# A depthwise causal convolution into a bilinear feed-forward: w3 transposed by DMA out of a bf16 copy in HBM instead of by TensorE

## The chip, the core and the metric

One core of a Trainium2 chip runs the whole kernel in one launch. The metric is device time in microseconds (us); less is better. The engines are named as in the profile: PE (TensorE, matmuls), PEld (its weight loads), DVE (VectorE), ACT (ScalarE), POOL (GpSimd) and SP (SyncE). POOL and SP also issue DMAs; what they issue runs on the same 16 DMA engines. In the profile POOL's DMAs are queue q0 and SP's are queue q1.

## The reference

```
w   = softmax(weight, axis=-1)                       # weight [8 heads, 7 taps]
y[b, s, h, g] = sum_k w[h, k] * xpad[b, s + k, h, g] # x [8, 3904, 192], 6 zero rows ahead; 192 = 8 heads x 24
X   = y.reshape(31232, 192)
out = (((X @ w1) * (X @ w2)) @ w3) @ w_out           # w1, w2 [192, 1024]; w3 [1024, 1024]; w_out [1024, 192]
```

All inputs and the output are float32. Because nothing nonlinear stands between `w3` and `w_out`, the kernel multiplies them first: W = w3 @ w_out, [1024, 192], and `out = (a * b) @ W`.

## The kernel before

The 31232 tokens are two halves (r = 0, 1) of 15616, worked on together. A half is cut in two ways. For the convolution it is cut into windows of 64 input rows that give 58 output rows each; 272 windows stand in ten blocks of 10, 10, 10, 32, 36, 36, 36, 36, 36 and 30 windows (`SIZES`). For the products it is cut into 31 rounds of 512 tokens.

- **`load_x(b)`** loads block b from HBM to SBUF, casting to bf16, by DMAs in POOL's queue. There are six buffers `xb`; blocks from 3 on use two each.
- **`conv(b, h0, nh)`** is the convolution of heads as matmuls with a band matrix, from `xb` into PSUM (`cps`), and copies it to `convo`. `conv_two` does two heads, and after the last two of a block calls `store(b)`.
- The feature dimension has to come onto the partitions. Blocks 0 to 2 are transposed on PE (`pe_transposes`). From window 26 on, `store` writes `convo` to a table `rows` in HBM (SP's queue), and `transposes(R)` reads it back for round R by three DMA transposes, also in SP's queue, into `xT`. `send(last)` issues the transposes of all rounds up to `last` whose rows are stored.
- **`first_product(R)`** makes a and b for the 8 groups `ft` of 128 features, 12 matmuls each; ACT copies a (`asb`), DVE multiplies it with b into `abT`. `abT` has three buffers.
- **`second_product(R, r)`** multiplies `abT` by W and writes 512 rows of `out` through ACT and SP.
- PSUM is one ring of four buffers (`banks`), taken in program order by every user.

The order of the work is written out by hand (a manual schedule). The start: 18 dummy matmuls (`warm`), the band matrix, block 0, `first_product(0)` with block 1 inside, `first_product(1)` with block 2 inside, `first_product(2)`. Then comes what is called the **W stage** below: for each of the eight row groups `jt` of w3, eight PE transposes of 128x128 (L404), their copy out of PSUM (L407, ACT and DVE in turn), and eight matmuls with `w_out` (`w3_product`, L413); the eight heads of block 3 are put between. After it stand the phases: phase 0 has four second products (rounds 0 and 1), each later phase two first products and then four second products. Block 4 and later blocks put four heads into a phase: a pair after the first second product (place 0) and a pair after the last (place 3).

POOL's queue in the start is: x of block 0, w1 and w2 up to column 768, x of block 1, copies that swap the halves of w1 and w2 (L332), the rest of w1 and w2, x of block 2, twelve more swap copies, `w_out`, eight loads of w3 (`w3b`, 128 rows each, cast to bf16), x of block 3, x of block 4. Each of POOL's DMAs signals one of eight semaphores in turn, and POOL waits for the DMA eight places earlier before it reuses one. From block 5 on a load is held back by a tiny copy (`pace`) that waits for a piece of `abT`.

Of the kernel before, what the change touches and what calls it, by code (L numbers as in the profile page):

```python
# [9 lines left out]
BF16 = mybir.dt.bfloat16  # L10
# [6 lines left out]
def kernel(  # L17
# [51 lines left out]
    def banks_bf16(name):  # L69
        return psum.tile([128, 16, 128], BF16, tag="banks", name=name)  # L70
# [18 lines left out]
    def load_x(b, parts=(0, 1)):  # L89
        tiles = xb_of.setdefault(b, [])  # L90
        zeros_of = zero_rows.setdefault(b, [])
        for i0, n in [v for e, v in enumerate(halves_of(b)) if e in parts]:
            xb = work.tile([128, n, D], BF16, tag="xb", bufs=6, name="xb")
            w = 0
            if i0 == 0:
                nc.vector.memset(xb[:, 0, :], 0.0)
                for r in range(NS):
                    nc.gpsimd.dma_start(out=xb[Q * r:Q * r + Q, 1:n, :], in_=x_spans(r, 1, n - 1))
                w = n
            while w < n:  # L100
                i = i0 + w
                m = min(n - w, WB - i % WB)
                at_end = i + m == NWIN
                if at_end:
                    m -= 1
                if m:
                    for r in range(NS):
                        nc.gpsimd.dma_start(out=xb[Q * r:Q * r + Q, w:w + m, :],  # L108
                                            in_=x_spans(r, i, m))
                if i % WB == 0:  # L110
                    zeros_of += [(xb, 0, w), (xb, 1, w)]
                w += m
                if at_end:
                    nc.gpsimd.memset(xb[Q:128, w, :], 0.0)
                    t = tok(NWIN - 1) - PAD
                    nc.gpsimd.dma_start(out=xb[0:Q, w, :], in_=x_rows[t:t + Q, :])
                    nc.gpsimd.dma_start(out=xb[Q:Q + PAD + LAST, w, :],
                                        in_=x_rows[TS + t:TS + t + PAD + LAST, :])
                    w += 1
            if len(halves_of(b)) == 1:  # L120
                tiles += [(xb, 0), (xb, SIZES[b] // 2)]
            else:
                tiles.append((xb, 0))
# [43 lines left out]
    def warm(n, t=None):  # L167
        t = banks("warm") if t is None else t
        for j in range(n):
            nc.tensor.matmul(t[:, j % 2, :], zeros[:, 0:128], zeros, start=True, stop=True)  # L170

    warm(18)


    wmax = const.tile([128, H], FP32)
# [153 lines left out]
    def swap_w(k, part, engines):  # L329
        cs = slice(WC[part], WC[part + 1])  # L330
        for f, (d, e) in zip(engines, ((0, Q), (Q, 0))):
            f(out=wsw[k][d:d + Q, cs], in_=wn[k][e:e + Q, cs])  # L332
# [7 lines left out]
    def first_product(R, between=None, lead=0):  # L340
        N = width(R)
        ab = work.tile([128, JT, NS, CH], BF16, tag="abT", bufs=LAG + 1, name="abT")
        abT_of[R] = ab
        r0 = (R * CH) % RING
        for ft in range(JT):
            pq = []
            for i in range(2):
                p = banks("pa" if i == 0 else "pb")
                pq.append(p)
                if ft == 0 and i == 0:  # L350
                    warm(lead, p)
                for k in range(NP):
                    for r in range(NS):
                        rs = slice(Q * r, Q * r + Q)
                        nc.tensor.matmul(  # L355
                            p[:, r, 0:N], w_of(i, k, r)[rs, ft * 128:(ft + 1) * 128],
                            xT[k][rs, r0:r0 + N],
                            start=(k == 0), stop=(k == NP - 1))
            pa, pb = pq
            asb = work.tile([128, NS, CH], BF16, tag="asb", bufs=3, name="asb")  # L360
            nc.scalar.copy(out=asb[:, :, 0:N], in_=pa[:, :, 0:N])  # L361
            nc.vector.tensor_tensor(out=ab[:, ft, :, 0:N], in0=asb[:, :, 0:N],  # L362
                                    in1=pb[:, :, 0:N], op=ALU.mult)
            if between and ft in between:
                between[ft]()

    def second_product(R, r):
        ab = abT_of[R]
        ng = width(R) // 128
        ops = banks("ops")  # L370
        for g in range(ng):
            for jt in range(JT):
                nc.tensor.matmul(  # L373
                    ops[:, g // 2, (g % 2) * D:(g % 2) * D + D],
                    ab[:, jt, r, g * 128:(g + 1) * 128], W_sb[:, jt, :],
                    start=(jt == 0), stop=(jt == JT - 1))
        osb = slot([128, ng, D], FP32, "osb")
        nc.scalar.copy(out=osb.rearrange("p (a g) d -> p a (g d)", g=2),  # L378
                       in_=ops[:, 0:ng // 2, 0:2 * D])
        t0 = r * TS + R * CH  # L380
        nc.sync.dma_start(
            out=out[t0:t0 + ng * 128, :].rearrange("(g p) d -> p g d", p=128), in_=osb)
        if r == 1:
            del abT_of[R]
# [1 line left out]

    W_sb = const.tile([128, JT, D], BF16)
    wo_b = const.tile([128, JT, D], BF16)
    w3r = moe_w3.rearrange("(jt jp) g -> jp jt g", jp=128)
    wor = moe_w_out.rearrange("(gt gp) d -> gp gt d", gp=128)  # L390
    w3b_of, w3T_of = {}, {}

    def load_wo():
        nc.gpsimd.dma_start(out=wo_b, in_=wor)

    def load_w3(jt):
        w3b_of[jt] = stage.tile([128, DFF], BF16, tag="w3b", bufs=JT, name="w3b")
        nc.gpsimd.dma_start(out=w3b_of[jt], in_=w3r[:, jt, :])

    def w3_transpose(jt, f):  # L400
        w3b = w3b_of.pop(jt)
        tps = banks_bf16("w3ps")
        for gt in range(JT):
            nc.tensor.transpose(out=tps[:, gt, :], in_=w3b[:, gt * 128:(gt + 1) * 128],  # L404
                                identity=ident)
        w3T_of[jt] = stage.tile([128, JT, 128], BF16, tag="w3T", bufs=3, name="w3T")
        f(out=w3T_of[jt], in_=tps[:, 0:JT, :])  # L407

    def w3_product(jt):
        w3T = w3T_of.pop(jt)  # L410
        wps = banks("wps")
        for gt in range(JT):
            nc.tensor.matmul(wps[:, 0, 0:D], w3T[:, gt, :], wo_b[:, gt, :],  # L413
                             start=(gt == 0), stop=(gt == JT - 1))
        nc.scalar.copy(out=W_sb[:, jt, :], in_=wps[:, 0, 0:D])

# [17 lines left out]
    for k, f in ((0, V), (1, A), (2, V)):  # L434
        move(f, pe_transpose(0, k))
    swap_w(1, 0, (V, A))
    load_x(2)
    for k in (0, 2, 1):
        swap_w(k, 1, (P, P))
    for k in (0, 2, 1):  # L440
        swap_w(k, 2, (P, P))
    load_wo()
    for jt in range(JT):
        load_w3(jt)
    load_x(3)
    load_x(4)

    def seq(*fs):
        def run():
# [10 lines left out]
        2: seq((conv, 2, 4, 4)),  # L460
        5: seq((pe_transposes, 2), (store, 2, 26))})
    first_product(2)

    def conv_two(b, h, engines):
        for j, f in enumerate(engines):
            conv(b, h + j, 1, (f,))
        if h + 2 == H:
            store(b)

    def send(last):  # L470
        while sent[0] <= last and min((sent[0] + 1) * CH, TS) <= stored[0]:
            transposes(sent[0])
            sent[0] += 1

    for jt in range(JT):
        w3_transpose(jt, A if jt % 2 == 0 else V)
        if 2 <= jt < 6:
            conv_two(3, 2 * (jt - 2), (V, A))
        if jt == 5:
            send(LAG + 4)  # L480
        if jt > 1:
            w3_product(jt - 2)
    w3_product(JT - 2)
    w3_product(JT - 1)


    phases = [()] + [(R, R + 1) for R in range(LAG + 1, NR, 2)]
    assert phases[-1][-1] == NR - 1
    pace = const.tile([1, 2], BF16)
    done = 0  # L490
    for p, rounds in enumerate(phases):
        b, e = PROLOGUE_BLOCKS + p // 2, p % 2
        if b < NB:
            for xb, r, w in zero_rows.pop(b, []):
                nc.gpsimd.memset(xb[Q * r:Q * r + PAD, w, :], 0.0)
        for j, R in enumerate(rounds):
            first_product(R)
            if j == 0 and b + 1 < NB:
                P(out=pace, in_=abT_of[R][0:1, JT - 1, 1, 0:2])  # L499
                load_x(b + 1, (0, 1) if p == 1 else (e,))  # L500
        last = NR if p == len(phases) - 1 else done + 2
        for i in range(done, last):
            second_product(i, 0)
            if b < NB and i == done:
                conv_two(b, 4 * e, (V, V))
            second_product(i, 1)
        done = last
        if b < NB:
            conv_two(b, 4 * e + 2, (V, V))
        send(min(NR - 1, LAG + 2 * p + 4))  # L510
    assert sent[0] == NR


# [28 lines left out]
```

## Time and profile before

| what | value |
|---|---|
| median of 3 runs (range) | 530.3 us (529.74 to 530.72) |
| the profiled execution | 530.57 us, of which its span on the core is 528.9 us |
| PE busy | 521.7 us, 99% of the span |
| DVE, ACT, POOL busy | 359.3, 316.2, 54.8 us |
| DMA bytes by queue, counted at the destination | q1 (SP) 45.65 MB, q0 (POOL) 16.63 MB |
| eight w3 loads, 256 KB each | median 8.7 us from issue to landing |
| 84 DMA transposes of `rows` | median 2.8 us from issue to landing |

PE is busy nearly without a hole, so what is on PE is mostly the time itself. Two things read from the page need care: it is an average over stages (the first 75 us have other limits than the rest), and bytes of casting DMAs are those written as bf16, half of the float32 that is read.

### The profile page before, as it was taken

To read this page: it belongs to the slowest core of one execution; us is meant where nothing else is said; L and a number is where in the kernel's file an instruction comes from. 1 tells how busy PE (TensorE), PEld (TensorE's weight loads), DVE (VectorE), ACT (ScalarE), POOL (GpSimd) and SP (SyncE) were. 2 spreads that over 40 slices of the span, in tenths; PEclk is the share of its full clock that TensorE was granted. 3 is DMA by queue.
4 is the path that set the end of the run, shared out by engine and by line. 5 is a ranking of instruction groups with operands and counts; after the bars stand their busy time and mean duration, and the time that the engine had idled before them with its cause. 6 is when DMAs were issued, how large, how long until landed. Compare 5 with 4: busy or idle time off the path is not lost.

```text
span 528.9 us, 12698 instructions
## 1 busy us (share of the span) xinstructions
PE 521.7 (99%) x5469; PEld 351.0 (66%) x5469; DVE 359.3 (68%) x337; ACT 316.2 (60%) x348; POOL 54.8 (10%) x102
## 2 busy tenths in 40 slices
PE   8999999999999999999999999999999999999996
PEld 4555975857658576585765857667585574846676
DVE  4779459397593976949669496794957849386460
ACT  3887557375573755737467374664746647375652
POOL 8841002011010100201001010020000000000000
PEclk9999999999999999999999999999999999999999
DMA  9999559979562894636956379554725055240204
GB/s 117 110 206 191 116 96 189 184 165 143 131 90 95 173 132 131 87 114 138 147 148 70 123 147 135 133 56 134 150 81 120 1 151 127 78 90 23 99 2 151
DMA packets 130541, 63.13 MB, mean 119 GB/s; under 512 B 83352, under 2 KB 129460, under 8 KB 130484
## 3 DMA queue, kind: packets, MB, share of 16 engines
q1 hardware_dynamic: 91764, 45.65, 35.7%
q0 software_dynamic: 38576, 16.63, 27.0%
q8 instruction: 43, 0.70, 0.6%
q14 instruction: 14, 0.11, 0.1%
q10 hardware_dynamic: 144, 0.03, 0.0%
HBM read 33.28 MB, written 34.82 MB: 129 GB/s over the span
## 4 chain that ended last, share of the span: by engine, by line
PE 96%; DVE 2%; ACT 1%; issue 0%; ACTq 0%
PE ops L373 31%; PE pa L355 30%; PE pb L355 29%; PE cps L249 2%; PE warm L170 1%; DVE abT L362 1%; ACT asb L361 1%; PE wps L413 1%; PE tps L302 1%; PE w3ps L404 0%; PE bps L215 0%; ACT convo L266 0%; DVE w3T L407 0%; DVE convo L423 0%; ACT osb L378 0%
## 5 line engine op out<-in xcount | busy, mean ns | idle before, releaser
L362 DVE TENSOR_TENSOR abT<-asb,pb 128x1024 bf16<-128x1024 bf16 (+1 forms) x248 | 298.3, 1204 | 45.8 <-ACT asb L361 29.3
L361 ACT CAST asb<-pa 128x1024 bf16<-128x1024 f32 (+1 forms) x248 | 247.6, 998 | 70.4 <-PE pa L355 69.7
L355 PE MATMUL pb<-xT,wn 64*128 64x512 bf16 (+1 forms) x744 | 201.8, 372 | 0.2
L355 PE MATMUL pa<-xT,wn 64*128 64x512 bf16 (+1 forms) x744 | 197.9, 373 | 0.5
L355 PE MATMUL pa<-xT,ws 64*128 64x512 bf16 (+1 forms) x744 | 198.0, 373 | 0.0
L355 PE MATMUL pb<-xT,ws 64*128 64x512 bf16 (+1 forms) x744 | 193.8, 373 | 0.0
L355 PEld LDWEIGHTS <-wn 64*128 64x128 bf16 x1488 | 138.7, 94 | 79.8 <-issue 4.8
L355 PEld LDWEIGHTS <-ws 64*128 64x128 bf16 x1488 | 129.0, 94 | 68.4 <-issue 3.3
L373 PEld LDWEIGHTS <-abT 128*128 128x128 bf16 x1952 | 159.7, 98 | 9.7 <-issue 9.7
L373 PE MATMUL ops<-W_sb,abT 128*128 128x192 bf16 x1952 | 165.7, 246 | 0.0
L378 ACT COPY osb<-ops 128x768 f32<-128x768 f32 (+1 forms) x62 | 48.8, 788 | 127.1 <-PE ops L373 127.1
L266 DVE CAST convo<-cps 128x864 bf16<-128x864 f32 (+7 forms) x65 | 52.0, 847 | 98.4 <-PE cps L249 96.8
L108 POOL DMA_DIRECT2D xb<-in_x_dram x38 | 29.9, 799 | 13.0 <-DMA w3b<-in_moe_w_dram 5.1
L499 POOL COPY pace<-abT 1x2 bf16<-1x2 bf16 x9 | 1.6, 175 | 266.2 <-DVE abT L362 266.2
L249 PE MATMUL cps<-xb,Aband 64*64 64x432 bf16 (+3 forms) x320 | 17.8, 309 | 0.4 <-DVE abT L362 0.2
L249 PEld LDWEIGHTS <-Aband 64*64 64x64 bf16 x320 | 5.8, 105 | 6.7 <-issue 5.7
L170 PE MATMUL warm<-zeros 128*128 128x512 bf16 x18 | 6.9, 572 | 1.4 <-DVE zeros L140 1.4
L266 ACT CAST convo<-cps 128x640 bf16<-128x640 f32 (+4 forms) x13 | 7.4, 606 | 0.8 <-PE cps L249 0.8
L332 POOL COPY ws<-wn 64x256 bf16<-64x256 bf16 (+1 forms) x16 | 7.2, 449 | 0.9
L413 PE MATMUL wps<-wo_b,w3T 128*128 128x192 bf16 x64 | 6.3, 246 | 0.1
L170 PEld LDWEIGHTS <-zeros 128*128 128x128 bf16 x20 | 2.5, 134 | 5.4 <-issue 3.8
L413 PEld LDWEIGHTS <-w3T 128*128 128x128 bf16 x64 | 5.1, 98 | 1.0 <-issue 0.7
(51 smaller groups left out, 59.6 us busy)
## 6 DMA issues: line engine op xcount, KB each, us to landing
out_dram<-osb SPq DMA_DIRECT2D x60, 384.0 KB, 3.0
xb<-in_x_dram POOLq DMA_DIRECT2D x14, 432.0 KB, 8.0
rows<-convo SPq DMA_DIRECT2D x7, 648.0 KB, 9.3
xb<-in_x_dram POOLq DMA_DIRECT2D x8, 384.0 KB, 10.5
w3b<-in_moe_w_dram POOLq DMA_DIRECT2D x8, 256.0 KB, 8.7
rows<-convo SPq DMA_DIRECT2D x3, 576.0 KB, 5.4
xT<-rows SPq DMA_TRANSPOSE x84, 2.8
rows<-convo SPq DMA_DIRECT2D x2, 540.0 KB, 8.8
```

Of the source, the lines that this page charges most:

```text
L108: nc.gpsimd.dma_start(out=xb[Q * r:Q * r + Q, w:w + m, :], in_=x_spans(r, i, m))
L170: nc.tensor.matmul(t[:, j % 2, :], zeros[:, 0:128], zeros, start=True, stop=True)
L249: nc.tensor.matmul(view(slice(Q * c, Q * c + Q), r)[:, :, j * G:(j + 1) * G], band_of(h, r), xb[Q * r:Q * r + Q, w0:w0 + n, h * G:(h + 1) ...
L266: f[e % len(f)](out=dst, in_=part)
L302: nc.tensor.transpose(out=tps[:, w, :], in_=convo[:, w, k].rearrange("p r g -> p (r g)"), identity=ident)
L332: f(out=wsw[k][d:d + Q, cs], in_=wn[k][e:e + Q, cs])
L355: nc.tensor.matmul(p[:, r, 0:N], w_of(i, k, r)[rs, ft * 128:(ft + 1) * 128], xT[k][rs, r0:r0 + N], start=(k == 0), stop=(k == NP - 1))
L361: nc.scalar.copy(out=asb[:, :, 0:N], in_=pa[:, :, 0:N])
L362: nc.vector.tensor_tensor(out=ab[:, ft, :, 0:N], in0=asb[:, :, 0:N], in1=pb[:, :, 0:N], op=ALU.mult)
L373: nc.tensor.matmul(ops[:, g // 2, (g % 2) * D:(g % 2) * D + D], ab[:, jt, r, g * 128:(g + 1) * 128], W_sb[:, jt, :], start=(jt == 0), stop ...
L378: nc.scalar.copy(out=osb.rearrange("p (a g) d -> p a (g d)", g=2), in_=ops[:, 0:ng // 2, 0:2 * D])
L413: nc.tensor.matmul(wps[:, 0, 0:D], w3T[:, gt, :], wo_b[:, gt, :], start=(gt == 0), stop=(gt == JT - 1))
```

## The change

w3 goes to SBUF in another way. Two DMAs in POOL's queue cast its two halves (512 rows each) from float32 to a bf16 copy `w3d` in HBM, and 16 DMA transposes in SP's queue read that copy into `w3T`: eight for each half, each 512 rows by 128 columns. The 64 PE transposes and the eight copies out of PSUM go. Further:

- The two casts stand earlier in POOL's queue than the eight loads did: one ahead of x of block 2, one in the middle of the twelve swap copies.
- x of block 4 is held back by a `pace` copy until the sixth group (ft = 5) of round 2 is in `abT`.
- The four pairs of heads of block 4 stood at places 0 and 3 of phases 0 and 1. They now stand at place 3 of phase 0 and at places 0, 2 and 3 of phase 1. Later blocks stay where they were.
- The W stage is now: for each `jt`, a pair of heads of block 3 (for jt below 4), then `w3_product(jt)`; `send` stands behind the stage.
- The start has 15 dummies instead of 18.

In SP's queue the 16 new transposes stand ahead of `store(2, 26)`, of `store(3)` and of the transposes of rounds 3 to 6.

```diff
-    warm(18)
+    warm(15)
...
-    w3r = moe_w3.rearrange("(jt jp) g -> jp jt g", jp=128)
-    w3b_of, w3T_of = {}, {}
+    w3d = dram.tile([DFF, DFF], BF16, name="w3d")
+    w3T = const.tile([128, JT, DFF], BF16)
+    HC = DFF // 2
-    def load_w3(jt):
-        w3b_of[jt] = stage.tile([128, DFF], BF16, tag="w3b", bufs=JT, name="w3b")
-        nc.gpsimd.dma_start(out=w3b_of[jt], in_=w3r[:, jt, :])
-
-    def w3_transpose(jt, f):
...
+    def load_w3(half):
+        rs = slice(half * HC, (half + 1) * HC)
+        nc.gpsimd.dma_start(out=w3d[rs], in_=moe_w3[rs])
+
+    def w3_transposes(half):
+        rs = slice(half * HC, (half + 1) * HC)
         for gt in range(JT):
+            nc.sync.dma_start_transpose(out=w3T[:, gt, rs], in_=w3d[rs, gt * 128:(gt + 1) * 128])
...
+    load_w3(0)
     load_x(2)
     for k in (0, 2, 1):
         swap_w(k, 1, (P, P))
+    load_w3(1)
     for k in (0, 2, 1):
         swap_w(k, 2, (P, P))
     load_wo()
-    for jt in range(JT):
-        load_w3(jt)
     load_x(3)
-    load_x(4)
+    w3_transposes(0)
+    w3_transposes(1)
+    pace = const.tile([1, 2], BF16)
+
+    def paced_x(b, parts, R, ft):
+        P(out=pace, in_=abT_of[R][0:1, ft, 1, 0:2])
+        load_x(b, parts)
...
     first_product(2)
+    paced_x(4, (0, 1), 2, 5)
...
     for jt in range(JT):
-        w3_transpose(jt, A if jt % 2 == 0 else V)
-        if 2 <= jt < 6:
-            conv_two(3, 2 * (jt - 2), (V, A))
-        if jt == 5:
-            send(LAG + 4)
-        if jt > 1:
-            w3_product(jt - 2)
-    w3_product(JT - 2)
-    w3_product(JT - 1)
+        if jt < H // 2:
+            conv_two(3, 2 * jt, (V, A))
+        w3_product(jt)
+    send(LAG + 4)
...
+    heads = [(b, h) for b in range(PROLOGUE_BLOCKS, NB) for h in range(0, H, 2)]
...
+        gaps = {0: (3,), 1: (0, 2, 3)}.get(p, (0, 3))
...
-        for i in range(done, last):
-            second_product(i, 0)
-            if b < NB and i == done:
-                conv_two(b, 4 * e, (V, V))
-            second_product(i, 1)
+        for i in range(NS * (last - done)):
+            second_product(done + i // NS, i % NS)
+            if i in gaps and heads:
+                conv_two(*heads.pop(0), (V, V))
         done = last
-        if b < NB:
-            conv_two(b, 4 * e + 2, (V, V))
         send(min(NR - 1, LAG + 2 * p + 4))
```

More of the change, by code (lines that the diff above doesn't have):

```diff
@@ L388 @@
     wo_b = const.tile([128, JT, D], BF16)
-    w3r = moe_w3.rearrange("(jt jp) g -> jp jt g", jp=128)
     wor = moe_w_out.rearrange("(gt gp) d -> gp gt d", gp=128)
-    w3b_of, w3T_of = {}, {}
+    w3d = dram.tile([DFF, DFF], BF16, name="w3d")
+    w3T = const.tile([128, JT, DFF], BF16)
+    HC = DFF // 2
     def load_wo():
         nc.gpsimd.dma_start(out=wo_b, in_=wor)
-    def load_w3(jt):
-        w3b_of[jt] = stage.tile([128, DFF], BF16, tag="w3b", bufs=JT, name="w3b")
-        nc.gpsimd.dma_start(out=w3b_of[jt], in_=w3r[:, jt, :])
-    def w3_transpose(jt, f):
-        w3b = w3b_of.pop(jt)
-        tps = banks_bf16("w3ps")
+    def load_w3(half):
[3 more added lines that the diff above has]
+        rs = slice(half * HC, (half + 1) * HC)
         for gt in range(JT):
[L404 to L407, printed above, removed]
+            nc.sync.dma_start_transpose(out=w3T[:, gt, rs], in_=w3d[rs, gt * 128:(gt + 1) * 128])
     def w3_product(jt):
-        w3T = w3T_of.pop(jt)
         wps = banks("wps")
         for gt in range(JT):
-            nc.tensor.matmul(wps[:, 0, 0:D], w3T[:, gt, :], wo_b[:, gt, :],
+            nc.tensor.matmul(wps[:, 0, 0:D], w3T[:, gt, jt * 128:(jt + 1) * 128], wo_b[:, gt, :],
                              start=(gt == 0), stop=(gt == JT - 1))
@@ L475 @@
     for jt in range(JT):
-        w3_transpose(jt, A if jt % 2 == 0 else V)
-        if 2 <= jt < 6:
-            conv_two(3, 2 * (jt - 2), (V, A))
-        if jt == 5:
-            send(LAG + 4)
-        if jt > 1:
-            w3_product(jt - 2)
-    w3_product(JT - 2)
-    w3_product(JT - 1)
+        if jt < H // 2:
+            conv_two(3, 2 * jt, (V, A))
+        w3_product(jt)
+    send(LAG + 4)
     phases = [()] + [(R, R + 1) for R in range(LAG + 1, NR, 2)]
     assert phases[-1][-1] == NR - 1
-    pace = const.tile([1, 2], BF16)
+    heads = [(b, h) for b in range(PROLOGUE_BLOCKS, NB) for h in range(0, H, 2)]
     done = 0
@@ L492 @@
         b, e = PROLOGUE_BLOCKS + p // 2, p % 2
-        if b < NB:
-            for xb, r, w in zero_rows.pop(b, []):
-                nc.gpsimd.memset(xb[Q * r:Q * r + PAD, w, :], 0.0)
+        gaps = {0: (3,), 1: (0, 2, 3)}.get(p, (0, 3))
+        for xb, r, w in zero_rows.pop(b, []):
+            nc.gpsimd.memset(xb[Q * r:Q * r + PAD, w, :], 0.0)
         for j, R in enumerate(rounds):
@@ L498 @@
             if j == 0 and b + 1 < NB:
-                P(out=pace, in_=abT_of[R][0:1, JT - 1, 1, 0:2])
-                load_x(b + 1, (0, 1) if p == 1 else (e,))
+                paced_x(b + 1, (0, 1) if p == 1 else (e,), R, JT - 1)
         last = NR if p == len(phases) - 1 else done + 2
-        for i in range(done, last):
-            second_product(i, 0)
-            if b < NB and i == done:
-                conv_two(b, 4 * e, (V, V))
-            second_product(i, 1)
+        for i in range(NS * (last - done)):
+            second_product(done + i // NS, i % NS)
+            if i in gaps and heads:
+                conv_two(*heads.pop(0), (V, V))
         done = last
-        if b < NB:
-            conv_two(b, 4 * e + 2, (V, V))
         send(min(NR - 1, LAG + 2 * p + 4))
-    assert sent[0] == NR
+    assert sent[0] == NR and not heads
 _INS = ['x', 'weight', 'moe_w1', 'moe_w2', 'moe_w3', 'moe_w_out']
```

## The prediction

> **What bounds the kernel now.** I read the page first (busy shares and the chain that ended last).
>
> ```profile
> PE 521.7 (99%) x5469; PEld 351.0 (66%) x5469; DVE 359.3 (68%) x337; ACT 316.2 (60%) x348; POOL 54.8 (10%) x102
> ...
> PE 96%; DVE 2%; ACT 1%; issue 0%; ACTq 0%
> ```
>
> PE holds 96% of the chain of 528.9 us: a microsecond taken off PE is a microsecond won, as long as nothing else comes late in its place. All that the change touches lies before 75 us, so next I read the chain in order of time there (start, length, what).
>
> ```profile
> 50.55 0.61 DVE w3T L407
> ...
> 53.69 0.45 PE w3ps L404 x8
> 54.14 0.47 PE cps L249 x8
> 54.61 0.77 PE wps L413 x8
> ...
> 71.81 0.49 PE cps L249 x8
> 72.30 0.75 PE pa L355 x6
> ```
>
> The W stage runs from 48.8 to 60.5 us. Its three kinds of work have one line each: eight transposes 0.45, a pair of heads 0.47, one `w3_product` 0.77. Round 3's first product begins at 72.2. The third view is the table by stretches, read for its last two columns (DMA share, GB/s at the destination).
>
> ```profile
> 19.40:22.20 2.80, 2.69 (x40) 1.37 (x36) 2.09 (x2) 2.79 (x4) 2.70 (x6) 1.00 0.01 1
> ...
> 24.90:34.90 10.00, 9.81 (x117) 5.04 (x114) 7.42 (x7) 8.74 (x11) 5.41 (x8) 1.00 1.13 209
> 34.90:43.50 8.60, 8.57 (x85) 4.89 (x84) 7.24 (x8) 6.89 (x9) 3.18 (x4) 1.00 1.55 197
> 43.50:53.50 10.00, 9.68 (x115) 6.34 (x111) 9.07 (x10) 8.09 (x10) 0.50 (x2) 1.00 1.62 187
> ...
> 54.50:58.00 3.50, 3.50 (x52) 3.08 (x49) 2.49 (x3) 3.12 (x7) 0.00 (x0) 1.00 0.04 7
> 58.00:67.20 9.20, 9.20 (x118) 8.70 (x117) 2.71 (x3) 3.23 (x7) 0.00 (x0) 1.00 0.78 166
> ```
>
> The DMA engines are full from 22 to 54 us (w3 in the second row, x of block 3 in the third, x of block 4 in the fourth) and from 58 on (stores of block 3). They idle only at 19.4 to 22.2 and 54.5 to 58, 6.3 us together. That is the room for 16 more DMAs.
>
> **The change part by part.** *PE transposes.* Eight times 0.45 = 3.6 us go. What stays is four pairs (2.0) and eight products (5.8 to 6.2), some 8.0 us. DVE's last product of round 2 ends at 50.55, and the ring of four PSUM buffers makes the third head wait for it; 0.7 to 1.0 us that lay under the transposes becomes visible. The stage takes 9.0 instead of 11.7: minus 2.7. The eight copies (L407: four at 1012 ns on ACT, four at 690 on DVE) were beside PE and win nothing more.
>
> *Dummies.* The first band sum needs the first `cprod`, ready at 7.46, and starts at 8.17, behind dummy 18. Three fewer can win 0 (if band sums then run at the slower pace of the first dummies, 0.43 us apart) to 0.7; I take 0.5, since the last dummies are already at the fast pace, from about 7.3 us.
>
> *Block 4's pair.* One pair (0.49) moves from phase 0 to phase 1: nothing in sum, but round 3 must be ready 0.5 sooner. Without other waits PE would reach round 3 at 72.2 - 0.5 - 2.7 - 0.5 = 68.5, and the end would come 3.2 us earlier.
>
> *POOL's queue.* A w3 load occupied POOL for 0.54 us (L398). The first cast, issued at 13.74 behind the last w1/w2 load, delays x of block 2 and the swap copies (twelve in 5.31 us from 15.29) by 0.55; the second delays the last six by 1.1. The last copy ended at 20.6, so 21.7; pb of group 6 wants it at 22.3, or 21.8 with the dummies gone. Cost 0; up to 0.5 if a cast takes POOL 1 us.
>
> *DMA time of the casts.* No row shows HBM to HBM. Bounds: the w3 loads (2.1 MB, 10.0 us at 209 GB/s), 5.0 us for a half, as the nearest row; below it nothing much, since the same float32 is read (4.5); above it 7.5, should writing HBM take half as long again, as the stores to HBM at 166 GB/s suggest against 209. I take 4.8 each. Half 0 moves from 15.4 to 20.2. x of block 2 (0.49 MB, 2.6 us at the full rate) follows to 22.8 and lands by 24; its convolution starts at 26.9 (26.4 after), 2.4 us of cover. Half 1 moves to 27.6.
>
> *The 16 transposes.* A row shows the like: `xT<-rows`, also 512x128. Alone they come every 1.25 to 1.3 us (SP's issue), and move 0.13 MB within 0.75 us. Against loads of x it is slower:
>
> ```profile
> DMA packets 1162, 0.38 MB, mean 174 GB/s; under 512 B 1162, under 2 KB 1162, under 8 KB 1162
> ...
> q0 software_dynamic: 669, 0.26, 94.7%
> q1 hardware_dynamic: 493, 0.13, 44.1%
> ```
>
> This is the DMA view from 121.9 to 124.1: one transpose took 2.2 us there, and the loads kept some 60% of their own rate. So 0.75 us of full DMA time each, 12 us in all, and 1.25 to 2.2 us apart. From 15.4 on the work up to the last transpose is 9.6 (casts) + 2.6 (x of block 2) + 2.0 (`w_out`) + 8.4 (x of block 3) + 12 = 34.6: it would end at 50 to 51.5, with the old idle stretch filled. But x of block 4 joins: DVE's sixth product of round 2 ends at about 48.0 (47.5 after), POOL issues, and data move from about 49.9. By then three or four transposes are left. At 1.3 us each the last lands at 53 to 55, at 2.2 at 57.5 to 59.5. `w3_product(4)` comes at 54.5, and its last matmul, which needs the sixteenth, 0.6 later. I take 55: no visible wait.
>
> The Trainium skill ("DMA: Bandwidth & Descriptors", Latency and other measured facts) gives DMA transposes an effective 261 GB/s. By that a transpose is 0.5 us of DMA time, an estimate of 8 us for sixteen; the last would land near 50 and the change be worth 0.5 to 1 us more. The sum keeps to the row.
>
> *SP's queue.* Behind the sixteen stand `store(2, 26)`, `store(3)` and round 3's transposes. In the trace block 3's stores went out at 57.6 (right after the last head's copy), and the third transpose of round 3 was issued at 68.0, its bytes moving until 70.8, landed by about 71.6: 0.6 us before PE wanted it, 14.0 us after the stores. Now the last head's copy ends at about 54.6 and SP is free then too. So 54.7 + 14.0 = 68.7, and x of block 4 is still loading beside the stores. There is a row for such a pair: from 35.1 to 36.1 stores got 0.14 MB/us beside x of block 3, where alone they get 0.166; the 9.2 us of stores become 10.9. Round 3 is ready at 70.4 and PE, there at 68.5, waits 1.9.
>
> *The pace.* Behind it on POOL are only x of block 4 (six issues, 4.5 us), two memsets and the next pace. Full rate is 9.3 us for these 1.77 MB; shared, it lands at 63 to 67, before place 3 of phase 0 (68). That is what the moved pairs cover.
>
> **Sum.** Round 3 at 70.4 instead of 72.2 is -1.8, the pair moved behind it +0.5: -1.3 us. 530.57 - 1.3 = 529.3 for a profiled execution, which stood 0.3 above the median of the runs: 529.0.
>
> **The rivals.** *All of it arrives in time:* stores and loads overlap better, since they go in opposite directions (the pair above moved 0.23 MB/us together, more than either alone). Then -3.2: 527.1. Against it: round 3 had only 0.6 us to spare.
>
> *SP's chain takes it all back:* the sixteenth transpose is issued one to two us later than I take it; stores at 55.7 to 57, round 3 at 71.4 to 72.7, so -0.3 to +1.0: 530.0 to 531.3, 530.6 in the middle. This is no change: within 0.2% (1.06 us), which is what a measurement of this kernel can tell.
>
> *The loads crowd out the transposes (slower):* x of block 3 and then of block 4 keep their 60%, a transpose takes 2.2 us throughout. Four to five are left at 49.9, the last lands at 59.5 to 61.5, `w3_product(4)` waits 4.5 to 6, and the stores go out at about 59.5, their transposes landing at 74.5. Round 3 is 2.3 late, plus 0.5: 533. It decides from a landing of 57.5 on. For it: the row at 122 us. Against: after x of block 3 (by about 45) the transposes have the engines to themselves. The Trainium skill ("TensorE: Matmul & The Clock Gate", Part 1) has PE's clock fall to half after an idle window of about 3.4 us; with a wait that long it would add an estimated 1 to 2 us. No run here shows it: the trace has no such hole.
>
> *The cast itself is slow (slower):* at 7.5 us a half x of block 2 lands at about 26.5, level with its convolution, and all DMAs behind the second cast are 5.4 later. The sixteenth transpose lands at about 62, the stores go out at 61, round 3 is ready at 76.3: +4.1 and +0.5, 535.
>
> **How the numbers follow.** My forecast, 529.0 (its own range 528.2 to 529.7): 0.33. All in time: 0.12. Taken back: 0.15. Crowded out: 0.29. Slow cast: 0.11. So faster 0.45, same 0.15, slower 0.40. The forecast is the likeliest case though slower is close behind, as the DMA budget is full to within 4 us at two places. The range takes in "all in time" (526.9) and "crowded out" with the lower end of "slow cast" (535.0); some 3% lie below it, 13% above.
>
> **What would show it.** Right: no L404; the W stage near 9 us; casts near 4.8 us each; the last `w3T` landed by 55; x of block 4 landed between 63 and 67; PE waiting under 2.5 us for `xT` at round 3; span near 527.6. Wrong: PE idle in the W stage before L413 products, released by `w3T<-w3d` (crowded out); casts over 6 us or a wait at block 2's convolution (slow cast); round 3 without a wait (all in time).

## The result, and the profile after

The change takes **534.54 us** (median of six runs, 532.37 to 536.17) against 530.38 us for the kernel before on the same chip: a ratio of 1.0076, 95% interval 1.0054 to 1.0098. It is slower by 4.2 us, where the prediction had it faster by 1.3. The profiled execution took 536.17 us, with a span of 534.5 us against 528.9; it is the slowest of the six, so the losses read from it add up to more than 4.2 us.

The page of the changed kernel (busy line of section 1, then the chain by engine and by line, then two groups):

```profile
PE 520.7 (97%) x5402; PEld 347.7 (65%) x5402; DVE 356.9 (67%) x333; ACT 312.8 (59%) x344; POOL 51.8 (10%) x97
...
PE 87%; SPq 6%; DMA 4%; POOL 2%; DVE 0%; issue 0%; ACT 0%; ACTq 0%; POOLq 0%
...
L249 PE MATMUL cps<-xb,Aband 64*64 64x432 bf16 (+3 forms) x320 | 18.4, 314 | 3.1 <-DMA xb<-in_x_dram 2.9
L409 PE MATMUL wps<-wo_b,w3T 128*128 128x192 bf16 x64 | 9.3, 315 | 3.2 <-DMA w3T<-w3d 3.2
```

PE lost 67 instructions in the trace, but only 1.0 us of busy time, and its share of the chain fell from 96 to 87%: SP's queue and the DMAs took the difference. The last two columns of the groups tell two things. PE sat idle 2.9 us for x of block 3 and 3.2 us for `w3T`. And one matmul of `w3_product` (L409) has a mean of 315 ns, where the same matmul took 246 ns before: the instruction did not change, so something slowed PE itself.

Where this lies is seen in PE's timeline from the start of the W stage (start, length, what; idle time before it and its releaser in brackets):

```profile
48.99 0.35 PE L249 MATMUL cps<-xb,Aband 64*64 64x384 bf16 x3
52.23 0.48 PE L249 MATMUL cps<-xb,Aband 64*64 64x384 bf16 x5 [2.88 <-DMA xb<-in_x_dram]
52.64 1.46 PE L409 MATMUL wps<-wo_b,w3T 128*128 128x192 bf16 x8
54.03 0.85 PE L249 MATMUL cps<-xb,Aband 64*64 64x384 bf16 x8
...
56.16 0.52 PE L249 MATMUL cps<-xb,Aband 64*64 64x384 bf16 x8
56.61 0.83 PE L409 MATMUL wps<-wo_b,w3T 128*128 128x192 bf16 x8
...
59.41 0.26 PE L409 MATMUL wps<-wo_b,w3T 128*128 128x192 bf16 x1 [0.30 <-DMA w3T<-w3d]
61.00 0.26 PE L409 MATMUL wps<-wo_b,w3T 128*128 128x192 bf16 x1 [1.33 <-DMA w3T<-w3d]
62.82 1.45 PE L409 MATMUL wps<-wo_b,w3T 128*128 128x192 bf16 x8 [1.56 <-DMA w3T<-w3d]
```

Four waits, 2.88 + 0.30 + 1.33 + 1.56 = 6.07 us. Eight matmuls of one `w3_product` take 0.83 us at 56.6, but 1.46 at 52.6, right behind the first wait, and 1.45 at 62.8, right behind the last. The table by stretches has the reason in its third column from the end, the granted clock of PE:

```profile
49.00:52.30 3.30, 0.42 (x9) 0.17 (x8) 1.64 (x2) 0.46 (x1) 3.30 (x6) 1.00 1.49 142
...
54.50:56.00 1.50, 1.50 (x16) 1.04 (x8) 1.02 (x2) 0.80 (x1) 0.00 (x0) 0.50 1.55 185
56.00:62.80 6.80, 3.63 (x41) 2.21 (x39) 1.92 (x2) 2.45 (x6) 0.50 (x2) 1.00 1.67 161
62.80:66.60 3.80, 3.78 (x26) 3.51 (x27) 0.00 (x0) 0.96 (x3) 0.00 (x0) 0.55 1.30 239
```

The clock falls to half twice (52.6 to 56.0 and 62.9 to 66.3 us, 3.41 us each in the trace's clock records). PE is busy 11.5 us in the stage; the same work at the full clock is 8.0 (no_transposes below). So the stage, from 49.0 to 66.6, is 8.0 of work + 6.1 of waits + 3.5 lost to the clock = 17.6 us, where it took 11.7: 5.9 us longer, and the span is 5.6 longer. One fall of 3.41 us takes 0.003 off the mean clock (an estimate); by that, the other five runs, at mean clocks of 0.994 to 0.997 against 0.993 here, had one or two.

The chain in order of time shows what the last wait hung on:

```profile
48.81 2.11 SPq L404
...
53.57 9.21 DMA w3T<-w3d
...
62.82 3.89 PE wps L409 x25
66.71 10.56 PE ops L373 x128
77.27 0.49 PE cps L249 x8
```

SP issued the sixteenth transpose at 53.6, close to the prediction, but its bytes landed at 62.8. Issued is not landed: several transposes stood in queue q1 behind each other. The DMA view from 41 to 48 us says how fast that queue moves beside the loads of x (packets, MB at the destination, share of the time):

```profile
q0 software_dynamic: 2016, 0.76, 87.1%
q1 hardware_dynamic: 2015, 0.48, 54.4%
```

The two queues move the **same number of packets**, 2016 and 2015. A packet of x is 384 bytes, one of a transpose 256 bytes, and a transpose has 512 of them, 0.131 MB (some of the counted packets are completion records of 4 bytes, so the bytes are the better measure). 0.48 MB are 3.7 transposes in 7 us, 1.9 us each. The loads of x get 0.76 MB / 7 us = 109 GB/s, 55% of the 197 they had alone. The Trainium skill ("DMA: Bandwidth & Descriptors", Queues, rings and completion order) says that a DMA engine goes round its queues packet by packet; these counts agree. By this, x of block 3 and the transposes delay each other until one of them is done.

### The profile page after: what moved, and what is told of

Same layout as the page of the kernel before. It is cut to its first block, busy times and chain, and to the rows that moved or that the text cites. A ratio compares the mean times of both kernels' runs of the same rounds, so it can differ in the third digit from the quotient of the medians.

```text
span 534.5 us, 12571 instructions
## 1 busy us (share of the span) xinstructions
PE 520.7 (97%) x5402; PEld 347.7 (65%) x5402; DVE 356.9 (67%) x333; ACT 312.8 (59%) x344; POOL 51.8 (10%) x97
## 4 chain that ended last, share of the span: by engine, by line
PE 87%; SPq 6%; DMA 4%; POOL 2%; DVE 0%; issue 0%; ACT 0%; ACTq 0%; POOLq 0%
PE ops L373 31%; PE pb L355 27%; PE pa L355 27%; SPq L404 6%; PE cps L249 2%; DMA w3T<-w3d 2%; DMA w3d<-in_moe_w_dram 2%; DMA wn<-in_moe_w_dram 1%; PE wps L409 1%; DVE abT L362 0%; POOL xb L98 0%; POOL ws L332 0%; POOL xb L129 0%; POOL wn L160 0%; POOL wn L161 0%
## 5 line engine op out<-in xcount | busy, mean ns | idle before, releaser
L409 PE MATMUL wps<-wo_b,w3T 128*128 128x192 bf16 x64 | 9.3, 315 | 3.2 <-DMA w3T<-w3d 3.2
L249 PEld LDWEIGHTS <-Aband 64*64 64x64 bf16 x320 | 5.8, 106 | 10.2 <-issue 9.7
L409 PEld LDWEIGHTS <-w3T 128*128 128x128 bf16 x64 | 7.3, 125 | 5.5 <-DMA w3T<-w3d 3.7
L411 ACT CAST W_sb<-wps 128x192 bf16<-128x192 f32 x8 | 2.6, 321 | 7.9 <-PE wps L409 7.9
L170 PE MATMUL warm<-zeros 128*128 128x512 bf16 x15 | 5.1, 515 | 1.4 <-DVE zeros L140 1.4
```

The costliest lines, as they stand in the source:

```text
L249: nc.tensor.matmul(view(slice(Q * c, Q * c + Q), r)[:, :, j * G:(j + 1) * G], band_of(h, r), xb[Q * r:Q * r + Q, w0:w0 + n, h * G:(h + 1) ...
L409: nc.tensor.matmul(wps[:, 0, 0:D], w3T[:, gt, jt * 128:(jt + 1) * 128], wo_b[:, gt, :], start=(gt == 0), stop=(gt == JT - 1))
```

## The experiments

The theory: two queues share the engines packet by packet, so sixteen transposes are late and make x of block 3 late; the clock adds its part. Rivals: the casts alone make everything late; or the small edits (dummies, pace, moved heads) cost the time. Ratios are to the kernel before on the same chip (530.42 to 530.65 us), with 95% intervals.

### half_transposes: the last eight transposes left out

```diff
-    w3_transposes(1)
...
-            nc.tensor.matmul(wps[:, 0, 0:D], w3T[:, gt, jt * 128:(jt + 1) * 128], wo_b[:, gt, :],
+            nc.tensor.matmul(wps[:, 0, 0:D], w3T[:, gt, (jt % 4) * 128:(jt % 4 + 1) * 128], wo_b[:, gt, :],
```

> The eight transposes of half 1 are left out (products 4 to 7 read half 0 again); both casts stay. Theory A: with half as many packets against it x of block 3 lands by 48.5 instead of 52.2, no wait over 0.5 us in the W stage, the stage takes 9 to 9.5, time 527.5 to 529. Theory B: both casts are as late as before, so x of block 3, queued behind them, still lands after 50.5 and PE waits 1.5 us or more for it; time 530 or more.

Measured: 528.19 us, ratio 0.9954 (0.9940 to 0.9969). PE's waits from 30 to 100 us:

```profile
PE pa L355 <- DMA xT<-rows: 1.2, 2, 0.9
PE cps L249 <- DMA xb<-in_x_dram: 0.4, 1, 0.4
PEld L355 <- DMA xT<-rows: 0.3, 1, 0.3
```

Both casts are still there (landed at 22.3 and 30.6, in the change at 23.4 and 32.1), and x of block 3 lands at 49.7 instead of 52.2, later than theory A had it (48.5) but sooner than theory B. The stage takes 8.2 us, the clock stays full. So the casts without the second eight transposes cost no time, and the whole loss hangs on what those eight add.

### no_transposes: no casts, w3 loaded as it is into `w3T`

```diff
-    load_w3(0)
-    load_w3(1)
...
+    for jt in range(JT):
+        nc.gpsimd.dma_start(out=w3T[:, jt, :], in_=moe_w3[jt * 128:(jt + 1) * 128, :])
...
-    w3_transposes(0)
-    w3_transposes(1)
```

> No casts to HBM and no transposes: w3 is loaded untransposed into w3T by eight DMAs where the kernel before has its loads, so the transposition is left out. Both theories: nothing is late in the W stage; this is the bound of what taking the transposes off PE can win. If the PE part of my sum was right the stage takes 9.0 (8.5 to 9.5) and the time is 527 to 528.5; if the store chain to round 3 takes part of it back, PE waits 1 to 2 us for xT at round 3 and it is 528.5 to 529.5. If the stage takes over 10, the PE part was wrong as well.

Measured: 528.57 us, ratio 0.9963 (0.9949 to 0.9976). The W stage takes 8.0 us (48.5 to 56.5), yet the kernel gains only 1.9 us, because PE then waits for `xT` at round 3: the stores' rows land at 64.8 and the third `xT` at 70.2. About 2 us is the most that taking w3 off PE can bring here.

### x4_late: x of block 4 paced behind the fourth product of the W stage

```diff
-    paced_x(4, (0, 1), 2, 5)
...
         w3_product(jt)
+        if jt == 3:
+            P(out=pace, in_=W_sb[0:1, 3, 0:2])
+            load_x(4)
...
-        gaps = {0: (3,), 1: (0, 2, 3)}.get(p, (0, 3))
+        gaps = {0: (), 1: (0, 1, 2, 3)}.get(p, (0, 3))
```

> x of block 4 waits for the fourth piece of W_sb (some 56 us) instead of the sixth group of round 2 (48 us), and its four pairs of heads all stand in phase 1. Theory A (shared engines: while loads of x are queued, the 16 DMA engines serve loads and transposes packet by packet, so each slows the other): the sixteenth w3T lands at 56 to 57 instead of 62.8, PE's waits for w3T go (3.2 us), the wait for x of block 3 (2.9) stays, PE's clock falls once instead of twice; W stage 12.5 to 13.5 instead of 17.6, time 529.5 to 531.5. Theory B (the casts to HBM are what is late; the transposes would be late without x of block 4 too): the sixteenth lands after 60, time 533 or more.

Measured: 541.66 us, ratio 1.0202 (1.0176 to 1.0228). In the W stage it did what the theory says: the last bytes of the sixteenth transpose have moved by 55.3 instead of 62.2, no wait for `w3T` is left, the wait for x of block 3 is 2.2 us, and the second products begin at 60.2 instead of 66.6. But x of block 4, now issued at 58 to 63, ran beside the transposes of round 3:

```profile
PE pa L355 <- DMA xT<-rows: 9.6, 3, 6.2
PEld L355 <- DMA xT<-rows: 6.5, 1, 6.5
PE cps L249 <- DMA xb<-in_x_dram: 2.2, 1, 2.2
```

Those waits, and 10.2 us at half clock from 75.5 on, cost more than the stage gained. It looks like the same sharing in another place: transposes that meet a load are late. My expectation of the time missed this.

### unpaced: x of block 4 right behind x of block 3, as before

```diff
     load_x(3)
+    load_x(4)
...
-    paced_x(4, (0, 1), 2, 5)
```

> The change without the pace: x of block 4 is issued right behind x of block 3. Theory A: x of block 3 ends at about 51 only, so its successor is held back by the queue, not by the pace: x of block 4 starts to move at 51 either way, w3T lands within 1 us of 62.8, time 533 to 536, the same as the change. Rival (the pace keeps x of block 4 off the transposes): the sixteenth w3T lands 2 us later or more, time 536.5 or more.

Measured: 537.28 us, ratio 1.0121 (1.0105 to 1.0137): some 2.5 us slower than the change. x of block 3 is less late (1.5 us), but the four waits for `w3T` grow to 6.3 us, although the sixteenth transpose is as late as in the change (last bytes at 62.4 against 62.2), not 2 us later as the rival had it. The time is the rival's, the landing theory A's. By the medians the pace of the change is worth having; the two profiled executions (536.68 and 536.17 us) differ by only 0.5.

### keep_clock: dummies that fill the waits

```diff
     first_product(2)
+    warm(13)
...
+        if jt == 4:
+            warm(18)
         w3_product(jt)
```

> 13 dummy matmuls ahead of block 3's first heads and 18 ahead of the fifth product, to fill PE's waits. Theory C (a third of the loss is PE's clock, which fell to half for two stretches of 3.4 us after the waits): data land as late as in the change (52.2 and 62.8), but the matmuls after the waits run at full rate; W stage 14 to 15 instead of 17.6, time 531 to 532.5. Rival: PE only waits longer for the same data, time 534 to 535.

Measured: 533.65 us, ratio 1.0056 (1.0039 to 1.0072). The data are as late as in the change (x of block 3 at 51.7), but the clock stays full in the whole stage:

```profile
51.70:64.20 12.50, 11.98 (x116) 7.70 (x115) 3.89 (x5) 5.23 (x12) 1.95 (x4) 1.00 1.48 187
64.20:75.40 11.20, 11.20 (x141) 10.70 (x140) 0.03 (x1) 3.14 (x5) 0.00 (x0) 1.00 1.11 198
```

Round 3 begins at 75.4 instead of 77.7, 2.3 us sooner: the clock's part between these two executions (some dummies last beyond the wait they fill). The waits stay. Between the medians only 0.9 us is left of it, since the profiled execution of the change is its slowest; 533.65 lies between the ranges of theory C and of its rival, so the clock was worth less than I expected.

### fewer_dummies and moved_only: the small edits without w3

The kernel before with 15 dummies:

```diff
-    warm(18)
+    warm(15)
```

> The kernel before with 15 dummies instead of 18, nothing else. If the dummies were in the way the band sums start 0.5 to 0.6 us sooner (7.6 instead of 8.2, as in the change's trace) and what of it reaches the W stage is 0.3 to 0.5 us: time 529.8 to 530.1. Rival: the swap copies and loads set the pace behind it and nothing reaches the end: 530.3 to 530.6.

Measured: 530.65 us, ratio 1.0005 (0.9996 to 1.0013). In its profiled execution the first products end 0.56 us sooner and the span is 0.6 shorter, but over eleven runs nothing measurable is left.

The kernel before with the paced x of block 4 and the moved heads:

```diff
-    load_x(4)
...
     first_product(2)
+    paced_x(4, (0, 1), 2, 5)
...
+        gaps = {0: (3,), 1: (0, 2, 3)}.get(p, (0, 3))
```

> The kernel before with two edits of the change alone: x of block 4 paced on the sixth product of round 2, and block 4's heads two places later. w3 stays with TensorE. The prediction's own terms: the pair moved behind round 3's first product leaves phase 0 by 0.5 us sooner, and round 3 cannot begin sooner than its xT (71.6), so 530.4 + 0 to 0.5 = 530.4 to 530.9. If the pace alone pushes x of block 4 into the stores of block 3 (57.6 on), those stores get some 0.14 MB/us, round 3's xT lands 1 to 2 us later and the time is 531.5 to 532.5.

Measured: 530.33 us, ratio 1.0001 (0.9992 to 1.0010). Neither costs anything that can be measured. The loss comes from w3.

### cast_rows and second_cast_rows: the casts in smaller DMAs

In cast_rows each cast is four DMAs of 128 rows; in second_cast_rows only the second one is, and its four pieces stand behind the swap copies.

```diff
-        nc.gpsimd.dma_start(out=w3d[rs], in_=moe_w3[rs])
+        for c in range(4):
+            r4 = slice(half * HC + c * 128, half * HC + c * 128 + 128)
+            nc.gpsimd.dma_start(out=w3d[r4], in_=moe_w3[r4])
```

> The change with each cast as four DMAs of 128 rows (2 KB written per row instead of pieces of 32 KB). Theory B (the casts as such come late: 8.9 and 12.9 us from issue to landing): smaller pieces let x of block 2 and the transposes in between, half 1 lands by 29.5 instead of 32.1, the transposes start to move 2 us sooner and the time falls to 532.5 or less. Theory A: the start moves by 1 us at most, and the pace of the transposes beside the loads (1.9 us each) stays; 533 to 536.

Measured: 533.24 us, ratio 1.0059 (1.0035 to 1.0083), with runs from 531.5 to 537.7. The profiled execution took 531.52 us and is among the fastest. A piece lands every 1.24 us, 5.0 for a half (in packets of 16 KB, not 2 KB); the halves are there at 22.2 and 30.0 instead of 23.4 and 32.1, hardly sooner than the same casts as in the change landed in half_transposes (22.3 and 30.6). POOL's swap copies came later for the extra issues, so the first products ended at 52.4 instead of 49.1, and x of block 4, which is paced by them, was issued 3.3 us later too. x of block 3 still landed at 52.1, but PE now came so late that it waited only 0.6 us for it; the transposes had no load beside them from 51.2 to 54.6, the sixteenth had moved by 55.9 instead of 62.2, and PE never waited for `w3T`. The stage took 8.1 us at full clock: the loss stood ahead of it.

```diff
-    load_w3(1)
...
+    for c in range(4):
+        r4 = slice(HC + c * 128, HC + c * 128 + 128)
+        nc.gpsimd.dma_start(out=w3d[r4], in_=moe_w3[r4])
     load_wo()
     load_x(3)
```

> The change with its second cast split into four DMAs of 128 rows, issued by POOL behind the swap copies (22.3 us) and ahead of w_out, so that no swap copy waits for them. In cast_rows such pieces took 1.24 us each, 5.0 for a half, where the second cast of the change took some 7.6 us of the engines; here the half then lands at about 30 in place of 32.1. If the slow casts are what makes all later transfers late, everything behind moves up by 2 to 2.5 us: x of block 3 at about 50 (wait under 1 us, no first clock fall), the sixteenth w3T at 60, and the time gains 3 to 4 us: 530.5 to 531.5. If the sharing between transposes and loads sets both landings and the casts matter little (cast_rows landed x of block 3 at 52.1 all the same), x of block 3 lands at 51 to 52, w3T at 62 and the time is 533 to 535, that of the change.

Measured: 536.52 us, ratio 1.0118 (1.0102 to 1.0135). The pieces queued behind x of block 2 (landed 26.9), so the half was there at 31.9, hardly sooner than in the change, and x of block 3 at 52.1, with waits of 2.3 us for it and 4.0 for `w3T`. This run did not move what it was to move; its time is above both ranges, and it does not decide between them.

### half_by_dma, half_x3_first, x3_first: other splits and orders

half_by_dma sends rows 0 to 511 of w3 through HBM (one cast, eight transposes); the rest is loaded and transposed on PE as before, x of block 4 unpaced.

```diff
+    def cast_w3():
+        nc.gpsimd.dma_start(out=w3d, in_=moe_w3[0:HC])
...
     load_x(2)
+    cast_w3()
...
-    for jt in range(JT):
+    for jt in range(HJ, JT):
         load_w3(jt)
     load_x(3)
+    w3_transposes()
```

> The kernel before, with half of w3 (row groups 0 to 3) transposed by DMA out of one cast to HBM that stands behind x of block 2, and the other half by PE as before; 18 dummies, x of block 4 not paced, block 4's heads where they were. Theory A (engines shared packet by packet): half as many new packets end before x of block 3 is needed; x of block 3 lands by 48, PE waits under 0.5 us in the W stage, which takes about 10 us instead of 11.7; time 528.3 to 529.5, faster than both kernels. Rival: every transpose that shares the engines with loads delays x of block 3 or round 3 by as much as PE saves; PE waits over 1 us at one of the two, time 530 to 531.5.

Measured: 532.88 us, ratio 1.0023 (1.0002 to 1.0043). `w3T` is in time, but x of block 3 shares with eight transposes and lands at 52.1: a wait of 3.4 us and one fall of the clock. Of its ten runs four took 529.3 to 530.3 at a mean clock of 0.998 to 1.0, six took 532.7 to 534.1 at 0.994 to 0.996: the runs with a lower mean clock are the slow ones. They are 3.4 us longer in the mean, of which their mean clock (0.9955 against 0.9995) makes 2.1, an estimate; what makes the rest is not shown, since only one run was traced.

half_x3_first loads x of block 3 ahead of the four w3 loads:

```diff
+    load_x(3)
     for jt in range(HJ, JT):
         load_w3(jt)
-    load_x(3)
```

> Half of w3 goes through HBM as in half_by_dma, the other half through TensorE; x of block 3 is loaded ahead of the four w3 loads of the second half instead of behind them. Theory A (two queues share the DMA engines packet by packet, 1.9 us a transpose beside loads): the cast lands near 25 as before, w_out near 29.5, then eight transposes and x of block 3 run side by side for some 15 us and both end by 46; the four w3 loads follow at 1.3 us each and land by 51, x of block 4 by 60. PE waits under 1 us in the W stage, the clock stays full, the stage takes 10 us in place of 11.7, round 3 begins near 70.6: 528.9 us (528.3 to 529.7), better than both kernels. Theory B (whatever stands behind a cast to HBM is late, in any order): x of block 3 still lands after 49 and the time stays at 532 to 533.

Measured: 538.17 us, ratio 1.0149 (1.0123 to 1.0175). My expectation failed, and its failure says most about the sharing. DMA view from 40 to 48 us:

```profile
q0 software_dynamic: 796, 0.82, 91.8%
q1 hardware_dynamic: 796, 0.19, 54.8%
```

Again the counts are equal, but q0 now also carries w3 rows in packets of 2 KB, and both queues move only 796 packets in 8 us. 0.19 MB are 1.45 transposes, 5.5 us each. The time of a transpose is not 1.9 us "beside loads": it grows with the size of the neighbour's packets. The last four w3 loads landed at 53 to 57 us instead of 51, and PE waited for x, for w3 and for `w3h` in turn.

x3_first is the change with the second cast issued behind x of block 3:

```diff
-    load_w3(1)
...
     load_x(3)
+    load_w3(1)
     w3_transposes(0)
```

> The change with one line moved: the second cast is issued behind x of block 3. Theory A: x of block 3 runs beside the first eight transposes and lands by 42 (52.2 in the change), so the 2.9 us wait and the first fall of the clock are gone; the second cast then runs to about 46 to 49, the last eight transposes run from there, most of them beside x of block 4 at 1.9 us, and the sixteenth lands at 61 to 64, as late as before: PE waits 4 to 7 us for w3T in front of the fifth product, with one clock fall. 532 us (530.5 to 534). Theory B (the wait for w3T is a matter of the casts being first in the queue): the later cast costs more, 536 or above. Theory C (the wait for x of block 3 is the whole loss): 530.5 or below.

Measured: 553.6 us, ratio 1.0405 (1.0349 to 1.0461), with runs from 548.4 to 557.7, the profiled one the slowest; in direction what the cast theory said, but for another reason: the cast was then in the queue beside the first half's transposes. DMA view from 44 to 64 us:

```profile
DMA  9000099009999098393005999209924690000999
...
q1 hardware_dynamic: 926, 0.22, 88.1%
q0 software_dynamic: 452, 0.94, 66.7%
```

The cast's packets are 32 KB and take 2.4 us or more each; in 20 us q1 moved 926 packets, less than two transposes. x of block 3 landed at 65.6, the cast at 68.5. The zeros in the first row are not idle engines: this view books a packet whole in the slice (0.5 us here) in which it starts, and the cast's packets took 2.4 to 6.5 us. Booked over their whole length, packets were in flight in every one of these slices. What equal turns do not explain is that q1 moved twice as many packets as q0, and that its packets took 0.30 us each (88.1% of 16 engines' 20 us, over 926), against 0.03 in the change from 41 to 48 us; what held them was not found.

## Why the prediction was wrong

**Right: PE's side.** The eight PE transposes are gone and the stage's work is 8.0 us (forecast 8.0, and 9.0 with a wait for PSUM that did not show: 8.0 and 8.2 in the two runs without late data).

**Right: the store chain as next limit.** Round 3's `xT` was to be ready at 70.4; no_transposes has it at 70.2. With all data in time the change would be worth 1.9 to 2.2 us (528.6 and 528.2), between "all in time" and the forecast.

**The step that failed: how many transposes were left, and at what pace.** The sum had three or four left at 49.9, 1.3 us each, and the last landing at 55. In the trace queue q1 had moved 1.20 MB by 49.9 (DMA view from 20 to 49.9 us), 9.2 transposes of 0.131 MB, so nearly seven were left, and they took 1.8 us each, since first x of block 3 and then x of block 4 shared the engines with them: the sixteenth landed at 62.8, where I wrote "I take 55: no visible wait". x4_late has the part of x of block 4 by itself: without it the last bytes had moved by 55.3 instead of 62.2. The prediction's other row, 2.2 us each against loads, was nearer than 1.3.

The prices were nearly right. "0.75 us of full DMA time each" came out as 0.86 (1.9 us at the 45% that the loads left), 13.7 us for sixteen in place of 12. A cast has two packets of 32 KB for each of the 16 engines, 2.43 us each when nothing disturbs them: 4.9 us for the second half (5.7 for the first, whose packets took up to 3.7), where I took 4.8. But the casts' last bytes moved at 23.0 and 31.8 us (21.9 and 30.2 in half_transposes) instead of 20.2 and 27.6, and from 24 to 32 us, beside the second cast, only half a transpose moved. Why the other queue moved so little there is not shown. And the idle time of the engines, 6.3 us, was called the room for sixteen DMAs that the same sum priced at 12 us.

**The deadline that was not checked: x of block 3.** It was due at 49. The sum let all work end at 50 to 51.5, which already was later, and never asked which transfer would be last among them. With equal turns the loads and the transposes beside them both end late. x of block 3 landed at 52.2 and cost 2.9 us, the first of the two falls of the clock not counted.

**The rival that came.** "The loads crowd out the transposes" had the mechanism, with 533 us. It put the last landing at 59.5 to 61.5 (62.8), the wait for `w3T` at 4.5 to 6 us (3.2), the stores at 59.5 (58.8). It lacked x of block 3 (2.9) and held the clock to a side sentence of 1 to 2 us, which became 3.5. Its argument against itself, that the transposes have the engines to themselves from about 45 on, did not hold: x of block 3 was there to 52, x of block 4 from 52 on. "The cast itself is slow" had late casts, and even gave 62 and 535, but not for its reason: a half took 4.9 to 5.7 us of the engines, not 7.5, and half_transposes, with casts nearly as late and no loss, shows that they alone are not enough. Whether sixteen transposes would fit behind casts that land sooner was not settled: second_cast_rows did not land its cast sooner, and in cast_rows PE itself came 3.3 us later.

**The clock.** It falls to half behind a wait and stays there for 3.41 us or a multiple. The Trainium skill ("TensorE: Matmul & The Clock Gate", Part 1) names windows of about 3.4 us; the length agrees. But the page has PE idle for a whole window before the fall, and here less was enough. The stretches at full clock are multiples as well (47.79 us = 14 x 3.413 from the first clock record of the change on), so in each trace the falls lie on a grid of 3.41 us, and the idle time within one window of that grid fits them, not the length of a wait. In the change the windows before the two falls had 2.88 us idle (49.2 to 52.6) and 2.90 (59.5 to 62.9), in x4_late 2.20 and in half_x3_first 2.15. The wait of 2.3 us in second_cast_rows brought no fall: it lay across two windows, 1.27 us idle in the one and 1.01 in the next. In all 14 traces every window at full clock with 2.15 us idle or more is followed by a fall (counted up to the end of the span), and none with 1.91 or less. This is read from the traces afterwards; no run moved a wait against the grid to test it.

**The small terms.** The dummies' 0.5 us left nothing that can be measured, the moved pair and the pace cost nothing (fewer_dummies, moved_only). In the change the first products ended at 49.1 in spite of fewer dummies, since the first products waited 0.9 us in all for POOL's swap copies (PE's weight loads, `ws`); the prediction had cost that at 0 to 0.5.

No version run here does all the work and beats the kernel before.

## What to carry to other kernels

Before moving work from PE to the DMA engines, add up the engine time it needs and hold that against the idle engine time before each deadline, for every transfer that shares the stretch and not only for the moved ones. Beside loads, the two queues here moved equal numbers of packets (2016 and 2015, 796 and 796), so a transfer in small packets is paced by its neighbour's packet size: price it beside the loads it will meet, not alone. A wait of two to three microseconds on PE can cost 1.7 us more through the clock (3.41 us at half).

## What the runs showed of the hardware that was not expected

- A DMA transpose of 512x128 took 1.9 us beside packets of 384 bytes (the change) and 5.5 us beside a mix with packets of 2 KB (half_x3_first); beside casts with packets of 32 KB fewer than two moved in 20 us (x3_first).
- A cast of 512 rows from HBM to HBM took about the same time of each engine as one DMA (packets of 32 KB, 2.43 us each; 4.9 us for the second cast of the change) and as four DMAs of 128 rows (packets of 16 KB, 1.23 us each; 5.0 us in cast_rows).
- The fall of PE's clock went by the idle time within windows of 3.41 us on a fixed grid: 2.15 us idle in one window brought it, a wait of 2.3 us split over two did not.
